# A scheduler that lets VectorE and GpSimd exclude each other, and an instruction order searched anew with it

## The chip, the core and the metric

The kernel runs on one core of one Trainium2 chip. The metric is the device time of one execution in microseconds (us). A core has five engines that run side by side and wait for each other through semaphores: TensorE (PE; its weight loads are shown apart as PEld), VectorE (DVE), ScalarE (ACT), GpSimd (POOL) and SyncE (SP), whose queue issues all DMAs of this kernel. The profile was taken in one execution; its span is the time from that execution's first instruction to its last.

## What is computed

An attention layer with soft-capped scores feeds a two-layer feed-forward block with a squared ReLU.

```python
scores = cap * tanh(scale * q @ k.T / cap)        # batch 4, heads 12, seq 448, head_dim 64
attn   = softmax(scores)                          # the row maximum is subtracted first
x      = (attn @ v) as [1792, 768]
h      = x @ w_in                                 # w_in [768, 2048]
g      = s * relu(h) ** 2 + b
out    = g @ w_out                                # w_out [2048, 768]
```

## The kernel before, in words

The work is cut into four batches j = 0 to 3 of 448 tokens. For each batch, attention runs over six pairs of heads. For a pair, TensorE computes blocks of scores (L505, into `ps_s`), ScalarE applies tanh (L509) and exp (L513), and TensorE multiplies the probabilities by the values and sums them (L563 and L571, into `ps_v`). ScalarE copies the result out (L591, `pw`), four small DMAs gather the row sums (L526, `cmp`), GpSimd and VectorE take their reciprocal (L534, L535, L538), a DMA writes it to DRAM (L540, `zd`), two DMAs read it back spread over partitions (L545), and one product (L437 on GpSimd) makes `num`, the reciprocal product. After six pairs a maximum is taken (L451, L609, L610), sent through TensorE so that all partitions have it (`lanes`, L470, one matmul of a single column), and x is split into a high half-precision part and a low part (L426 or L427, then L446).

The feed-forward weights arrive as 64-bit floats. VectorE rearranges their bits (L655, L656), an engine multiplies by a power of two (`expo`, L429 on GpSimd), and VectorE joins the bits (L659). Squares of the input weights (L693, L694 or L695, one instruction for each of three pieces of a column group) are summed by 12 small matmuls (`norm`, L705); a `lanes` matmul and a short VectorE sequence (`fin`, L721 to L726) give the scale, and the weights are split into high and low parts too. The output weights go the same way in `wout`; their column sums (L436 or L437) end in one matmul (L778).

The first product (L835, L836, L837) makes 16 blocks of 18 matmuls for each batch, the second (L1086 to L1088) six blocks of 48 for batches 0 and 1. Batches 2 and 3 use a form with fewer products (L995). After each block of the first product, ScalarE applies relu and square (L848, L853), a conversion makes the high part (`ghi`, L429 on GpSimd) and a subtraction the low part (`glo`, L437 on GpSimd).

No order is written by hand. Every instruction group is registered with a cost for each engine that may run it, a rank, its inputs and outputs. `Plan.emit` then plays the program through a model of the five engines and emits the groups in the order in which that model starts them; each engine executes its own part strictly in that order. The ranks come from the table `CHOICE["at"]`, the engines that an operation may use from entries such as `'expo'` or `'glo'`. Operations registered with `port=True` disturb each other in the model when VectorE and GpSimd run them at the same time:

```python
        loss = {"DVE": 0.9, "POOL": 0.7}
...
            if e in port and self.more[i][0]:
                other = port["POOL" if e == "DVE" else "DVE"]
                dur += max(0.0, min(other - t, dur)) * loss[e]
                port[e] = t + dur
```

Of the kernel before, what the change touches and what calls it, by code (L numbers as in the profile page):

```python
# [23 lines left out]
class Plan:  # L24
# [55 lines left out]
    def emit(self):  # L80
        n = len(self.ops)
# [31 lines left out]
        busy = {}  # L113
# [10 lines left out]
        shy = CHOICE["shy"]  # L124
        cold = 0.0
        kind = 0
        cling = CHOICE["cling"]

        def when(i, eng):
            ways, _, r, w, _ = self.ops[i]  # L130
            late = self.more[i][1]
            t = busy[eng]
            if eng == "SP" and len(landed) >= 8:
                t = max(t, landed[-8] - 0.4)
            for d in deps[i]:
                if start[d] is None:
                    return None
                t = max(t, end[d] + (0.0 if ran[d] == eng == "PE" else after[ran[d]] + before.get(eng, 0.0) + late))
# [4 lines left out]
            for p, ks in need.items():  # L143
                h, c = head[p], len(free[p])
                if set(order[p][h:h + len(ks)]) != ks:
                    return None
                for x in range(h, h + len(ks)):
                    if free[p][x % c] is None or taken.get((p, x % c)):
                        return None
                    t = max(t, free[p][x % c])  # L150
            for e, (dur, _) in ways.items():
                if e != eng and max(busy[e], t) + dur + shy.get(e, 0.0) + self.bias < t + ways[eng][0] + shy.get(eng, 0.0):
                    return None
            return t

        moved = 0.0
        landed = []
        port = {"DVE": 0.0, "POOL": 0.0}
        loss = {"DVE": 0.9, "POOL": 0.7}
        out = []  # L160
        todo = n
        while todo:
            best = None
            for reach in (80, n):
                for e, q in queue.items():
                    pick = None
                    for i in q[:reach]:
                        if pick and pick[0] <= busy[e] and self.ops[i][1] > self.ops[pick[1]][1] + cling:
                            break
                        t = when(i, e)  # L170
# [17 lines left out]
            t, i, e = best  # L188
            ways, _, r, w, move = self.ops[i]
            for other in ways:  # L190
                queue[other].remove(i)
            dur = ways[e][0]
# [18 lines left out]
            if e in port and self.more[i][0]:  # L211
                other = port["POOL" if e == "DVE" else "DVE"]
                dur += max(0.0, min(other - t, dur)) * loss[e]
                port[e] = t + dur
# [23 lines left out]
def arrange(units, at):  # L238

    key = {}  # L240
    for name, pre, _ in units:
# [4 lines left out]
CHOICE = {  # L246
    'bias': 1.798,
    'shy': {'DVE': 0.3, 'POOL': 0.5},
# [31 lines left out]
    },  # L280
    'alias': 2,
    'direct': 6,
    'cslag': 21,
    'late': 0.56,
    'lag': 0.0,
    'cling': 21.776,
    'parts': ((0, 1), (2, 3)),
# [5 lines left out]
    'sq': ('ACT', 'DVE', 'POOL'),  # L293
    'expo': ('POOL',),
    'whi': ('ACT', 'DVE'),
    'ohi': ('POOL',),
    'xhi': ('ACT', 'DVE'),
    'xmul': ('POOL',),
    'relu': ('ACT',),
    'gsq': ('ACT',),  # L300
    'glo': ('POOL',),
    'ghi': ('POOL',),
    'ehi': ('ACT', 'DVE', 'POOL'),
# [15 lines left out]
def attention_moe_kernel(  # L319
# [196 lines left out]
    def normal(bb, c2, rank):  # L516
# [19 lines left out]

        gps(0.4, rank, whole, r=["guard", *((kc, h, i) for h in range(2) for i in range(2))], w=[kc])
        dve(0.32, rank, lambda: nc.vector.reciprocal(P[kc][:, 0], P[kc][:, 0]), w=[kc])  # L538
# [14 lines left out]
    def pv(bb, c2, rank, step):  # L553
# [54 lines left out]
        def gather():  # L608
# [5 lines left out]
            gather,  # L614
            r=[("xm", bb, c) for c in range(NP)], w=[("xn", bb)],
        )
# [62 lines left out]
    def win(g, rank):  # L679
# [47 lines left out]

        dve(1.75, rank, fin, r=[kl], w=[("wnm", g), ("wc", g)])
        for c in range(NC3):
# [13 lines left out]
    def wout(d, rank):  # L743
# [44 lines left out]
        def amax():  # L788
# [4 lines left out]
        dve(  # L793
            0.68, rank, amax, r=[("wc", g) for g in range(NG)] + [("om", d, q) for q in range(NQ)], w=[("om", d)]
        )
# [5 lines left out]

        dve(1.3, rank, fin, r=[kl], w=[("op", d), ("os", d)])
        half = NQ // 2
# [60 lines left out]
    def mix(p, rank, step):  # L864
# [10 lines left out]

        dve(0.6, rank, scales, r=[("os", x) for x in d], w=[("ms", p)])
        for e in range(2):
# [379 lines left out]
```

## Time and profile before

| | before |
|---|---|
| median of 3 runs | 644.26 us (644.21 to 645.55) |
| the profiled execution, its own time | 644.03 us |
| its span | 642.2 us |
| PE busy | 627.1 us, 98% |
| DVE busy | 397.6 us, 62% |
| ACT busy | 326.6 us, 51% |
| POOL busy | 273.8 us, 43% |
| mean granted TensorE clock | 0.997 of full speed |

Busy time is the time in which an engine executes; what is missing to the span is idle time. The time of an execution is longer than its span by what lies around the first and the last instruction, here 1.83 us.

### The profile page before, as it was taken

What the parts mean: (1) busy time and instruction counts of PE and PEld (TensorE: products, weight loads), DVE (VectorE), ACT (ScalarE), POOL (GpSimd) and SP (SyncE); (2) the same over time, 40 slices, a digit from 0 to 9 for tenths busy, and PEclk for the clock granted to TensorE, in tenths of its full rate; (3) what the DMA queues carried; (4) which work ended last, traced back from release to release, by engine and by line L of the source; (5) the groups of instructions that cost most, each with busy time, mean ns of one, the idle gap of its engine ahead of it and who ended that gap; (6) DMA issues with size and microseconds to landing.
All of it is one profiled execution on the core that took longest, in us unless ns stands there. A gap on an engine that the chain in (4) does not pass through costs nothing.

```text
span 642.2 us, 11452 instructions
## 1 busy us (share of the span) xinstructions
PE 627.1 (98%) x4404; PEld 331.4 (52%) x4404; DVE 397.6 (62%) x778; ACT 326.6 (51%) x423; POOL 273.8 (43%) x319
## 2 busy tenths in 40 slices
PE   6999999999999999999999999999999999999997
PEld 2333344443334443333544445555558997556997
DVE  5896789997487787787400584745976222666222
ACT  5999987467866547537353561435544001434100
POOL 4553446885566568566343851112834001221000
PEclk9999999999999999989999999999999999999999
DMA  7767355441465674672800216676502875000672
GB/s 289 282 206 216 104 160 157 131 142 47 133 201 153 219 260 122 226 245 83 288 27 1 93 43 234 242 277 212 210 2 68 256 259 168 25 2 3 217 255 72
DMA packets 54775, 101.67 MB, mean 158 GB/s; under 512 B 16193, under 2 KB 34753, under 8 KB 54721
## 3 DMA queue, kind: packets, MB, share of 16 engines
q1 hardware_dynamic: 54720, 100.95, 47.1%
q8 instruction: 34, 0.56, 0.3%
q14 instruction: 21, 0.16, 0.1%
HBM read 82.58 MB, written 18.17 MB: 157 GB/s over the span
## 4 chain that ended last, share of the span: by engine, by line
PE 77%; DVE 8%; DMA 7%; POOL 3%; issue 2%; SPq 1%; ACT 0%; POOLq 0%; ACTq 0%
PE ps_m L995 9%; PE ps_s L505 7%; PE ps_s L995 6%; PE ps_v L563 6%; PE ps_s L836 6%; PE ps_s L837 6%; PE ps_s L835 6%; PE ps_m L1086 5%; PE ps_m L1088 5%; PE ps_m L1087 5%; PE ps_m L835 4%; PE ps_m L837 4%; PE ps_m L836 4%; PE ps_v L571 3%; DMA w<-in_w_in 2%
## 5 line engine op out<-in xcount | busy, mean ns | idle before, releaser
L995 PEld LDWEIGHTS <-w 128*128 128x128 f16 x1008 | 96.6, 98 | 0.7
L509 ACT ACTIVATE bed<-ps_s,arena 128x896 f32<-128x896 f32 x84 | 81.6, 1007 | 16.0 <-PE ps_s L505 14.8
L505 PE MATMUL ps_s<-bed 64*128 64x448 f32 (+1 forms) x384 | 82.7, 590 | 3.3 <-DMA bed<-in_qT 2.6
L513 ACT ACTIVATE bed<-bed,par 128x896 f32<-128x896 f32 x84 | 84.5, 1041 | 0.4
L563 PE MATMUL ps_v<-bed 128*32 128x448 f32 x768 | 82.2, 545 | 0.2 <-ACT pw L591 0.2
L1086 PE MATMUL ps_m<-gt,w 128*128 128x448 f16 x192 | 67.7, 353 | 0.0
L835 PE MATMUL ps_m<-x,w 128*128 128x448 f16 x192 | 67.7, 353 | 0.0
L836 PE MATMUL ps_s<-x,w 128*128 128x448 f16 x192 | 67.7, 352 | 0.0
L1088 PE MATMUL ps_m<-gt,w 128*128 128x448 f16 x192 | 67.7, 352 | 0.0
L837 PE MATMUL ps_m<-x,w 128*128 128x448 f16 x192 | 67.7, 352 | 0.0
L1087 PE MATMUL ps_m<-gt,w 128*128 128x448 f16 x192 | 67.7, 352 | 0.0
L835 PE MATMUL ps_s<-x,w 128*128 128x448 f16 x192 | 67.7, 352 | 0.0
L837 PE MATMUL ps_s<-x,w 128*128 128x448 f16 x192 | 67.7, 352 | 0.0
L836 PE MATMUL ps_m<-x,w 128*128 128x448 f16 x192 | 67.7, 352 | 0.0
L835 PEld LDWEIGHTS <-w 128*128 128x128 f16 x384 | 37.6, 98 | 38.7 <-issue 4.2
L837 PEld LDWEIGHTS <-w 128*128 128x128 f16 x384 | 37.6, 98 | 35.1
L836 PEld LDWEIGHTS <-w 128*128 128x128 f16 x384 | 37.6, 98 | 33.7
L429 POOL TENSOR_SCALAR w<-w 128x512 f32<-128x512 f32 x42 | 35.0, 833 | 40.0 <-DVE w L656 31.9
L930 ACT ACTIVATE pw<-ps_s,arena 128x448 f32<-128x448 f32 x32 | 20.3, 633 | 60.9 <-PE ps_s L837 57.8
L505 PEld LDWEIGHTS ps_s<-bed 64*128 64x128 f32 (+1 forms) x384 | 27.3, 177 | 45.4 <-issue 15.8
L437 POOL TENSOR_TENSOR pw<-pw 128x224 f32<-128x224 f32 x16 | 13.7, 860 | 79.5 <-ACT pw L934 63.1
L563 PEld LDWEIGHTS ps_v<-bed 128*32 128x32 f32 x768 | 20.5, 109 | 52.4 <-issue 38.6
(138 smaller groups left out, 1065.3 us busy)
## 6 DMA issues: line engine op xcount, KB each, us to landing
w<-w SPq DMA_DIRECT2D x48, 512.0 KB, 5.5
w<-in_w_out SPq DMA_DIRECT2D x24, 512.0 KB, 5.5
w<-ws SPq DMA_DIRECT2D x24, 512.0 KB, 4.7
w<-in_w_in SPq DMA_DIRECT2D x18, 512.0 KB, 5.4
bed<-in_v SPq DMA_DIRECT2D x24, 256.0 KB, 3.5
ws<-w SPq DMA_DIRECT2D x12, 512.0 KB, 2.9
bed<-in_kT SPq DMA_DIRECT2D x24, 224.0 KB, 3.8
bed<-in_qT SPq DMA_DIRECT2D x24, 224.0 KB, 3.8
```

What stands on the lines that cost most here:

```text
L429: 0.1 + n * 0.00107, lambda: nc.gpsimd.tensor_scalar(dst(), src(), sc, 1.0, ALU.mult, ALU.mult)
L505: nc.tensor.matmul(P[kp][o, h, 0:S], keys, P[q][rows], start=True, stop=True)
L509: 1.01, rank, lambda: nc.scalar.activation(P[kh], P[kp][:, :, 0:S], AF.Tanh, scale=tsc[:, 0:1]),
L513: 1.04, rank, lambda: nc.scalar.activation(P[kh], P[kh], AF.Exp, scale=par[:, 0:1]), r=["par"], w=[kh],
L563: nc.tensor.matmul(P[kp][o, 0, 0:S], P[kv][:, c, o], prob(c, h), start=(c == 0), stop=(c == NC))
L835: nc.tensor.matmul(ps[:, 0:S], wh, x[:, 0], start=(c == 0), stop=False)
L836: nc.tensor.matmul(ps[:, 0:S], wh, x[:, 1], start=False, stop=False)
L837: nc.tensor.matmul(ps[:, 0:S], wl, x[:, 0], start=False, stop=(c == NP - 1))
L995: nc.tensor.matmul(at(), w(g, zw), b(g, zb), start=g == 0 and x == 0, stop=g == n - 1 and x == 2,)
L1086: nc.tensor.matmul(ps[:, 0:S], wh, ghi[:, f], start=(f == 0), stop=False)
L1087: nc.tensor.matmul(ps[:, 0:S], wh, glo[:, f], start=False, stop=False)
L1088: nc.tensor.matmul(ps[:, 0:S], wl, ghi[:, f], start=False, stop=(f == NF - 1))
```

## The change

The model's charge for two disturbing operations is replaced. An operation with `port=True` that starts while the other engine's last such operation still runs is now held up until that one's end, less 0.15 us, and then takes its full own time. The choice between engines counts this hold-up too, and the scheduler looks through the whole queue of ready work where it looked at the first 80 entries first. Five more groups of operations are marked `port=True`. Four kinds of operation may run on more engines than before, and the table of ranks and three numbers beside it are new. What the instructions compute is the same.

```diff
-            for e, (dur, _) in ways.items():
-                if e != eng and max(busy[e], t) + dur + shy.get(e, 0.0) + self.bias < t + ways[eng][0] + shy.get(eng, 0.0):
-                    return None
+            if len(ways) > 1:
+                own = ways[eng][0] + held_up(i, eng, t)
+                for e, (dur, _) in ways.items():
+                    at = max(busy[e], t)
+                    if e != eng and at + dur + held_up(i, e, at) + shy.get(e, 0.0) + self.bias < t + own + shy.get(eng, 0.0):
+                        return None
             return t
+
+        def held_up(i, e, t):
+            if e not in port or not self.more[i][0]:
+                return 0.0
+            return max(0.0, port["POOL" if e == "DVE" else "DVE"] - t - 0.15)
...
-        loss = {"DVE": 0.9, "POOL": 0.7}
...
-            for reach in (80, n):
+            for _ in range(1):
                 for e, q in queue.items():
                     pick = None
-                    for i in q[:reach]:
+                    for i in q:
...
-                other = port["POOL" if e == "DVE" else "DVE"]
-                dur += max(0.0, min(other - t, dur)) * loss[e]
+                dur += held_up(i, e, t)
...
-    'bias': 1.798,
+    'bias': 1.806,
...
-        ('a', 0, 0): (-15.1, 72.6), ('a', 0, 2): (69.2, 7.69), ('a', 0, 4): (78.0, 15.05), ('a', 1, 0): (600.1, 1.25),
+        ('a', 0, 0): (-88.4, 62.61), ('a', 0, 2): (80.2, 2.4), ('a', 0, 4): (227.3, 40.55),
...
-    'late': 0.56,
+    'late': 0.621,
-    'cling': 21.776,
+    'cling': 19.274,
...
-    'expo': ('POOL',),
+    'expo': ('DVE', 'POOL'),
-    'ohi': ('POOL',),
+    'ohi': ('ACT', 'DVE', 'POOL'),
-    'xmul': ('POOL',),
+    'xmul': ('DVE', 'POOL'),
-    'glo': ('POOL',),
-    'ghi': ('POOL',),
+    'glo': ('DVE', 'POOL'),
+    'ghi': ('ACT', 'DVE', 'POOL'),
...
-        dve(1.75, rank, fin, r=[kl], w=[("wnm", g), ("wc", g)])
+        dve(1.75, rank, fin, r=[kl], w=[("wnm", g), ("wc", g)], port=True)
```

The diff makes the file longer by 7 to 8 lines, so that a line number of the kernel before stands 7 to 8 higher in the rows of the changed kernel below.

TensorE executes the same 4404 matmul records as before. GpSimd executes 81 instructions fewer, ScalarE 49 and VectorE 32 more. The larger moves are these: of 32 conversions `gt<-r` (`ghi`) on GpSimd 23 go to ScalarE and 4 to VectorE; of 32 subtractions `gt<-r,gt` (`glo`) on GpSimd 19 go to VectorE; of 48 high parts of the output weights (`ohi`) on GpSimd 19 go to ScalarE and 7 to VectorE; of 48 `expo` products on GpSimd 10 go to VectorE; of 24 reciprocal products on GpSimd 7 go to VectorE.

Three places show how the order moves. The first is the beginning of the SP queue, from its first DMA on (`in_kT` and `in_qT` are the keys and queries of one pair of heads, `par` holds the three scalars of the input). Before:

```order
L1132 DMA par<-in_cap 128x1
L481 DMA bed<-in_kT 128x448
L483 DMA bed<-in_qT 128x448
L647 DMA w<-in_w_in 128x1024 x3
L1132 DMA par<-in_s 128x1
L1132 DMA par<-in_b 128x1
L481 DMA bed<-in_kT 128x448
L483 DMA bed<-in_qT 128x448
L487 DMA bed<-in_v 128x512
L647 DMA gt<-in_w_in 128x1024
```

In the changed kernel, from the same instruction on:

```order
L1140 DMA par<-in_cap 128x1
L488 DMA bed<-in_kT 128x448
L490 DMA bed<-in_qT 128x448
L654 DMA w<-in_w_in 128x1024 x3
L488 DMA bed<-in_kT 128x448
L490 DMA bed<-in_qT 128x448
L1140 DMA par<-in_s 128x1
L1140 DMA par<-in_b 128x1
L494 DMA bed<-in_v 128x512 x2
L654 DMA gt<-in_w_in 128x1024
```

The keys and queries of the second pair have moved ahead of the two scalars s and b, and the second load of values ahead of a piece of weights.

The second place is VectorE's work just before it reads the third `norm` result (the third L713, which becomes L720). Before, with the bit join of the last piece (L659) and the squares (L694):

```order
L655 TENSOR_SCALAR gt<-gt 128x512
L656 SCALAR_TENSOR_TENSOR gt<-gt 128x512
L538 RECIPROCAL cmp<-cmp 128x7
L659 SCALAR_TENSOR_TENSOR gt<-gt 128x512
L451 TENSOR_REDUCE arena<-num 128x1
L694 TENSOR_TENSOR bed<-w 128x512 x2
L713 TENSOR_REDUCE arena<-ps_m 128x1
```

In the changed kernel (L662, L663, L434 and L666 are the bit work with its product, L701 the square):

```order
L662 TENSOR_SCALAR gt<-gt 128x512
L663 SCALAR_TENSOR_TENSOR gt<-gt 128x512
L434 TENSOR_SCALAR gt<-gt 128x512
L545 RECIPROCAL cmp<-cmp 128x7
L666 SCALAR_TENSOR_TENSOR gt<-gt 128x512
L701 TENSOR_TENSOR bed<-gt 128x512
L701 TENSOR_TENSOR bed<-w 128x512 x2
L720 TENSOR_REDUCE arena<-ps_m 128x1
```

The power-of-two product and the square of the last piece `gt`, both on GpSimd before, now stand on VectorE between its own instructions.

The third place is on TensorE, where the `lanes` matmul of batch 1 (L470, which becomes L477) stands. Between the last value matmul of batch 1 and this one stood 18 first-product matmuls, nine score blocks and four value steps of later pairs; the last of them are shown:

```order
L505 MATMUL ps_s<-bed 128x448 x2
L563 MATMUL ps_v<-bed 32x448 x8
L571 MATMUL ps_v<-bed,ones 32x448
L571 MATMUL ps_v<-bed,half 32x448
L571 MATMUL ps_v<-bed,ones 32x448
L571 MATMUL ps_v<-bed,half 32x448
L505 MATMUL ps_s<-bed 128x448 x2
L470 LDWEIGHTS ones_132
L470 MATMUL ps_m<-brief,ones_132 128x1
L835 LDWEIGHTS w_6_127
L835 MATMUL ps_m<-x,w_6_127 128x448
```

In the changed kernel 36 matmuls of the first product (L842 to L844 and their like, of which the last is shown) stand directly ahead of it:

```order
L845 LDWEIGHTS w_6_127
L845 MATMUL ps_m<-x,w_6_127 128x448
L477 LDWEIGHTS ones_132
L477 MATMUL ps_m<-brief,ones_132 128x1
L512 MATMUL ps_s<-bed 128x448 x2
L785 MATMUL ps_m<-arena,bed 128x1
L512 MATMUL ps_s<-bed 128x448 x2
L477 LDWEIGHTS ones_132
L477 MATMUL ps_m<-brief,ones_132 128x1
```

Between the last value matmul of batch 1 and this one now stand 144 first-product matmuls, eight score blocks (a row of four is two blocks of two) and two value steps. The column sum of the first output block (L778, now L785) follows it after one score block.

## Rows read from the trace of the kernel before

**Rows 1.** Stretches: length, busy PE, PEld, DVE, ACT, POOL; clock, DMA, GB/s

```profile
0.00:14.00 14.00, 9.16 (x34) 3.24 (x38) 6.44 (x11) 6.75 (x8) 5.52 (x16) 1.00 0.75 271
14.00:80.00 66.00, 64.14 (x556) 21.20 (x552) 51.98 (x116) 61.73 (x70) 31.25 (x40) 1.00 0.65 209
80.00:180.00 100.00, 98.87 (x694) 42.06 (x694) 82.87 (x162) 72.14 (x96) 64.23 (x71) 1.00 0.43 135
180.00:310.00 130.00, 126.02 (x863) 50.41 (x856) 104.39 (x225) 75.46 (x84) 85.99 (x112) 0.99 0.56 183
310.00:638.00 328.00, 328.00 (x2263) 213.84 (x2262) 151.43 (x264) 110.52 (x168) 86.81 (x82) 1.00 0.41 141
638.00:642.20 4.20, 0.91 (x10) 0.66 (x7) 0.45 (x1) 0.00 (x0) 0.00 (x0) 1.00 0.21 79
```

**Rows 2.** TensorE's own waits: for whom, us in total, times, longest

```profile
PE ps_m L778 <- POOL bed L437: 2.5, 1, 2.5
...
PE ps_m L470 <- DVE brief L715: 0.8, 2, 0.5
```

**Rows 3.** Timeline, 3.5 to 14 us, with what ended the idle time before

```profile
3.54 0.44 SPq L1132 DMA_DIRECT2D par<-in_s  x1
4.03 0.63 SPq L1132 DMA_DIRECT2D par<-in_b  x1
...
5.40 0.43 SPq L483 DMA_DIRECT2D bed<-in_qT  x1
...
12.50 0.97 PE L505 MATMUL ps_s<-bed 64*64 64x448 f32 x4 [1.93 <-DMA bed<-in_qT]
...
13.40 1.71 PE L563 MATMUL ps_v<-bed 128*32 128x448 f32 x16
```

**Rows 4.** DMA throughput in 40 slices of 0.5 us, from 0 to 20 us

```profile
GB/s 0 0 0 0 36 90 165 381 391 363 385 426 401 401 410 401 164 49 4 259 373 387 433 431 417 392 397 417 433 418 418 410 393 410 418 381 389 377 405 418
```

**Rows 5.** Timeline around the third sum of squares, 60 to 68 us

```profile
60.12 0.70 DVE L659 SCALAR_TENSOR_TENSOR gt<-gt 128x512 int32<-128x512 int32 x1
...
64.11 1.15 POOL L437 TENSOR_TENSOR num<-pw,bed 128x448 f32<-128x448 f32 x1
...
64.20 1.60 DVE L659 SCALAR_TENSOR_TENSOR gt<-gt 128x512 int32<-128x512 int32 x1 [0.46 <-POOL gt L429]
...
65.95 1.04 POOL L695 TENSOR_TENSOR bed<-gt 128x512 bf16<-128x512 f32 x1 [0.69 <-DVE gt L659]
...
67.05 0.35 PE L705 MATMUL ps_m<-ones,bed 128*128 128x1 bf16 x8 [1.24 <-POOL bed L695]
```

**Rows 6.** Timeline of TensorE at the lanes matmul of batch 1

```profile
183.72 0.16 PE L470 MATMUL ps_m<-brief,ones 128*128 128x1 bf16 x1 [1.41 <-DVE brief L610]
183.75 0.35 PE L835 MATMUL ps_m<-x,w 128*128 128x448 f16 x1
183.94 0.35 PE L836 MATMUL ps_m<-x,w 128*128 128x448 f16 x1
```

**Rows 7.** The chain that ended last, at 42 and 275 us: start, us, what

```profile
41.61 1.71 PE ps_s L505 x8
43.31 1.64 PE ps_v L563 x16
...
45.71 1.87 PE ps_s L505 x12
...
274.72 3.27 PE ps_s L505 x12
```

**Rows 8.** The stretch behind the wait of 2.45 us, columns as in Rows 1

```profile
274.90:278.40 3.50, 3.50 (x16) 0.70 (x12) 3.13 (x13) 1.37 (x2) 2.23 (x5) 0.51 0.67 181
```

**Rows 9.** Groups of instructions: shapes, count, busy us, mean ns, idle before

```profile
L436 DVE TENSOR_TENSOR gt<-pw,gt 128x448 f16<-128x448 f32 x23 | 14.7, 639 | 3.2 <-ACT gt L426 2.6
...
L437 POOL TENSOR_TENSOR gt<-r,gt 128x448 f16<-128x448 f32 x32 | 38.3, 1200 | 1.2
...
L426 ACT ACTIVATE gt<-pw 128x448 f16<-128x448 f32 x11 | 6.1, 572 | 4.5 <-POOL pw L437 2.8 <-DVE pw L436 1.2 <-PE ps_m L1088 0.3
```

More of the change, by code (lines that the diff above doesn't have):

```diff
@@ L535, in whole @@
             nc.gpsimd.tensor_scalar(a, a, guard[:, 0:1], 0.0, ALU.add, ALU.add)
-        gps(0.4, rank, whole, r=["guard", *((kc, h, i) for h in range(2) for i in range(2))], w=[kc])
+        gps(0.55, rank, whole, r=["guard", *((kc, h, i) for h in range(2) for i in range(2))], w=[kc], port=True)
         dve(0.32, rank, lambda: nc.vector.reciprocal(P[kc][:, 0], P[kc][:, 0]), w=[kc])
@@ L614, in pv @@
             gather,
-            r=[("xm", bb, c) for c in range(NP)], w=[("xn", bb)],
+            r=[("xm", bb, c) for c in range(NP)], w=[("xn", bb)], port=True,
         )
@@ L793, in wout @@
         dve(
-            0.68, rank, amax, r=[("wc", g) for g in range(NG)] + [("om", d, q) for q in range(NQ)], w=[("om", d)]
+            0.68, rank, amax, r=[("wc", g) for g in range(NG)] + [("om", d, q) for q in range(NQ)], w=[("om", d)],
+            port=True,
         )
@@ L800, in fin @@
             nc.vector.tensor_scalar(sc, wn, si, None, ALU.mult)
-        dve(1.3, rank, fin, r=[kl], w=[("op", d), ("os", d)])
+        dve(1.3, rank, fin, r=[kl], w=[("op", d), ("os", d)], port=True)
         half = NQ // 2
@@ L874, in scales @@
             nc.vector.tensor_scalar(rs, iswo[:, d[0]:d[1] + 1], top[:, 0:1], None, ALU.mult)
-        dve(0.6, rank, scales, r=[("os", x) for x in d], w=[("ms", p)])
+        dve(0.6, rank, scales, r=[("os", x) for x in d], w=[("ms", p)], port=True)
         for e in range(2):
```

59 rows, old and new, of the table CHOICE are left out of this document.

## The prediction

> **What bounds the kernel now.** I read the busy time by stretch first [rows 1]. TensorE is busy for 328.00 of 328 us from 310 to 638 us: there the kernel can't get faster by a change of order. Before 310 us it stands still for little: 14 - 9.16 = 4.84 us in the first 14 us, then 1.86, 1.13 and 3.98 us in the next three stretches (66 - 64.14, 100 - 98.87, 130 - 126.02), and 4.20 - 0.91 = 3.29 us at the very end. The sum is 15.10 us. The busy time itself is dense: in the first product one matmul starts 0.19 us after the other [rows 6]. TensorE executes the same 4404 matmuls after the change, so only these 15.10 us can shrink, and what a stall costs afterwards through the clock. The same rows show what the other engines can spare: ScalarE is busy 61.73 of 66 us in the second stretch, and 72.14 of 100 in the third; VectorE 82.87 of 100 in the third.
>
> Next come the waits of TensorE themselves. In the head, the score block that serves the rest of the sequence of two pairs together waits 1.93 us for the second pair's queries, which were issued at 5.40 us behind the two scalars s and b [rows 3]. Around 8 to 9.5 us the DMA engines move 164, 49 and 4 GB/s where they move about 400 before and behind [rows 4]. The third sum of squares waits 1.24 us for a square on GpSimd [rows 5]. The lanes matmul of batch 1 waits 1.41 us [rows 6]. The column sum of one output block waits 2.45 us, shown rounded as 2.5 [rows 2], and behind it the granted clock stands at 0.51 of full speed for 3.5 us, which is the lower of the two levels, 1.2 GHz [rows 8]; 12 score matmuls take 3.27 us there that take 1.87 elsewhere [rows 7], so that this stall has a second price of 1.40 us. The mid waits are 1.86 + 1.13 + 3.98 = 6.97 us; with the clock 8.37.
>
> **How VectorE and GpSimd meet.** The wait of 1.24 us can be followed back [rows 5]. The bit join L659 takes 0.70 us at 60.12. At 64.20 it takes 1.60: a GpSimd product that began at 64.11 runs until 65.26, so 1.06 us of it are left. The new charge gives 0.70 + 1.06 - 0.15 = 1.61 us, the old one 0.70 + 0.9 x 0.70 = 1.33. The new one is right here, the old one 0.27 us too low; the square on GpSimd starts after the join and TensorE after the square. The Trainium skill (SBUF — State Buffer, section "SBUF: two separate sides") says that the two engines share a port pair as an exclusive lock: the one that starts first keeps it for its whole instruction. The trace agrees in this place, 1.60 us. By that rule alone every such collision is foreseen by the new model and the 3.82 us that I keep below would go, ending at 635.8; by the rows they stay, since only this one wait is traced to a collision.
>
> **The change part by part.**
>
> The head. Keys and queries of the second pair go ahead of s and b. If the slow 1.5 us belong to the two scalars, the scores no longer wait: -1.93 us. But the first values now stand behind both scalars, and the value matmuls, which began at 13.40 [rows 3], need them. Two loads of 128 x 448 numbers of four bytes at 400 GB/s take 1.15 us; 8.0 + 1.15 + 1.5 + 0.65 for 128 x 512 values gives 11.3 as the earliest start, 13.40 as the latest. I take the middle, -0.9 us (bounds -1.93 and 0).
>
> The third sum of squares. The product and the square of the late piece stand on VectorE, no hand-over to GpSimd is left, and the square stands ahead of two others that the sum doesn't need. -1.24 us (bound 0, if that VectorE chain is late).
>
> The lanes matmul of batch 1. Before, there lay 18 x 0.19 + 9 x 0.855 + 4 x 2.40 = 20.7 us of TensorE work between the last values and it (a score block is half of 1.71 us; a value step with its sums lasts from 43.31 to 45.71 [rows 7]), and it was 1.41 us too little. Now it is 144 x 0.19 + 8 x 0.855 + 2 x 2.40 = 39.0 us. -1.41 us (bound 0).
>
> The rest of the mid waits and the clock: 8.37 - 1.24 - 1.41 = 5.72 us, at places such as the column sums and the lanes matmuls [rows 2]. All 32 groups of this sort (18 lanes, 8 sums of squares, 6 column sums) stand elsewhere now, so this is drawn again. The bounds are 0 and the whole 5.72. The model's view of collisions is better; its view of DMAs, which end other such chains, is the old one. I let two thirds stay: 3.82 us, a gain of 1.90.
>
> New waits that the rows let me price. The first lanes matmul has two score blocks ahead of it since its sum of squares, 1.71 us, where a value step stood there too; three short VectorE steps fit, but one long one such as L659 at 0.70 to 1.60 us more does not: 0 to 1.3 us, I take 0.5. For the 49 instructions that ScalarE gets I take another 0.5 us: in the third stretch ten conversions of 0.572 us [rows 9] and some six others of about 0.6 come to 9.4 us on top of 72.14 of 100, which leaves it room on average but not at each place (bounds 0 and the second rival). Together +1.0.
>
> The low parts cost nothing on the path: 19 subtractions leave GpSimd at 1.200 us for VectorE at 0.639 [rows 9], which covers them with idle time of 17.13 us in the third stretch and 25.61 in the fourth [rows 1]; if that cover were gone, each would delay a second product by at most 0.639. Freed time on GpSimd is worth something only where a wait ends on it. After 310 us no stall is there to remove, and with 176.57 us idle on VectorE of 328 I see none to add: 0. The end is the same code with the same last block: 0.
>
> The sum: -0.9 - 1.24 - 1.41 - 1.90 + 1.0 = -4.45 us on the span of 642.2 gives 637.75, and with the 1.83 us that lie around it 639.6 us. (The profiled execution's own time, 644.03, lies 0.23 under the median of 644.26.) No more than 1.93 + 8.37 = 10.30 can come off: 631.9 + 1.83 = 633.7 us is the floor.
>
> **The rivals.**
>
> Nothing gained but the head. The new order loses at its own places what the old one lost at its own, 8.37 us with the clock, since waits of this kind come mostly from DMA chains whose price didn't change: the wait of batch 1, for one, is the end of a chain of three DMAs. Then -0.9 to 0 remain: 643.1 to 644.0 us. For it: only 1.24 of 6.97 us is traced to a collision. Against it: 39.0 us of cover in place of 20.7 is in the program, whatever the model thought.
>
> ScalarE becomes late (slower). Its relu frees the two PSUM buffers of the first product, and the ten conversions of batch 0 now run on the same engine between tanh and exp of the attention. It decides from the point where ScalarE work ahead of a relu is longer than one block of matmuls, 18 x 0.19 = 3.4 us: then TensorE stands. If half of the ten conversions come through, 2.9 us, and two of these stalls bring the clock down, 2 x 1.40, the span is 5.7 us longer than in the rival above: 649 us, and 646 with a quarter of them and one clock drop. Against it: 18.5 us are still idle of 100.
>
> The planner's new order is much better than I grant: all of 8.37 and 1.5 of the head go, 632.3 + 1.83 = 634.2 us.
>
> **How the numbers follow.** I call a difference within 0.2%, 1.3 us, no change: what a measurement of this kernel can just tell. The forecast has a chance of 0.62, ScalarE late 0.12, nothing but the head 0.19, everything gone 0.07. The forecast's own range comes from its bounds: the third of the drawn term could be all or nothing (-3.8 to +1.9), the head -1.0 to +0.9: 636.4 to 642.6. The range of 8 in 10 leaves out below it the last rival, and above it the longer half of ScalarE's: 636.4 to 645.0. Faster holds the forecast, the last rival and a little of the rival that ends at 643.1 (the border is 642.97): 0.70. Same holds most of that rival: 0.17. Slower 0.13.
>
> **What would show it.** In the changed profile: no wait of TensorE for the queries in the first 14 us, and value matmuls before 13.4 us; no wait at the third sum of squares and none at the lanes matmul of batch 1; mid waits of 3 to 5 us in place of 6.97 by the stretch table, and one clock drop or none; long VectorE steps seldom over twice their own time. It is wrong if waits before 310 us sum to 6 us or more, if relu on ScalarE ends TensorE's waits, or if TensorE stands still between 310 and 638 us.

## The result, and the profile after

The changed kernel takes **638.57 us** (median of 19 runs, 635.98 to 644.37), the kernel before 644.52 us in the same series (19 runs, 641.89 to 648.27): a ratio of 0.9917 with a 95% interval of 0.9898 to 0.9936. The profiled execution took 639.61 us and spans 637.8 us, 4.4 us less than the one before. The medians lie further apart, by 5.95 us. A difference that the two profiles don't show is how often the clock drops: the mean granted clock of each execution is on record, and one drop to half for 3.4 us in some 640 makes it 0.997. It is 0.997 or less in 52 of 68 executions of the kernel before (taken beside e1 to e12, one slow one left out), and in 8 of 25 of the changed kernel (this series and e11). Both profiled executions are among these. In the series of the changed kernel the five executions with such a drop have a median of 641.48 us, the other fourteen 638.46. All lines of the changed kernel that the prediction named stand some 7 lines further down (L705 is L712, L470 is L477, L778 is L785).

The stretches, to be read against [rows 1] (length, busy time of PE, PEld, DVE, ACT, POOL, then clock, DMA share, GB/s):

```profile
0.00:14.00 14.00, 10.02 (x46) 3.49 (x50) 6.38 (x12) 7.43 (x9) 4.26 (x14) 1.00 0.81 293
14.00:80.00 66.00, 63.27 (x527) 20.19 (x519) 53.69 (x113) 58.91 (x67) 29.24 (x35) 0.97 0.65 204
80.00:180.00 100.00, 100.00 (x700) 43.64 (x693) 77.08 (x190) 81.57 (x112) 40.27 (x49) 1.00 0.41 134
180.00:310.00 130.00, 129.19 (x914) 51.23 (x912) 106.13 (x237) 84.48 (x103) 67.21 (x83) 1.00 0.59 184
310.00:634.00 324.00, 324.00 (x2233) 212.61 (x2232) 156.46 (x259) 119.28 (x185) 67.13 (x59) 1.00 0.43 144
634.00:637.80 3.80, 0.53 (x6) 0.27 (x3) 0.45 (x1) 0.00 (x0) 0.00 (x0) 1.00 0.14 50
```

TensorE's idle time is 3.98, 2.73, 0, 0.81, 0 and 3.27 us, 10.79 in all; before it was 4.84, 1.86, 1.13, 3.98, 0 and 3.29, 15.10. The difference of 4.31 us is the difference of the spans but for 0.1. So the gain lies in 80 to 310 us (4.30 us) and the head (0.86), and 14 to 80 us lost 0.87. GpSimd is busy 40 instead of 64 us in the third stretch, ScalarE 82 instead of 72.

TensorE's waits, to be read against [rows 2] (for whom, us in total, times, longest):

```profile
PE ps_m L1163 <- POOL w L1166: 2.1, 1, 2.1
PE ps_m L712 <- DVE bed L701: 1.7, 1, 1.7
PE ps_s L512 <- DMA bed<-in_qT: 1.6, 2, 1.0
PE ps_m L785 <- DVE bed L443: 0.8, 2, 0.6
PE ps_v L570 <- ACT pw L598: 0.6, 1, 0.6
PE ps_s L512 <- ACT bed L516: 0.3, 1, 0.3
PE ps_m L477 <- DVE brief L722: 0.3, 1, 0.3
```

The first of them, 2.08 us at the very start for a GpSimd memset, is as long in the kernel before. Of the column sums one waited 2.45 us; now two wait, 0.23 and 0.58. The largest wait behind the start is now the third sum of squares, 1.66 us against 1.24 [rows 5]; the granted clock falls behind it:

```profile
59.73 0.43 DVE L662 TENSOR_SCALAR gt<-gt 128x512 int32<-128x512 int32 x1 [1.71 <-DMA gt<-in_w_in]
...
61.91 1.14 POOL L444 TENSOR_TENSOR num<-pw,bed 128x448 f32<-128x448 f32 x1
62.00 1.62 DVE L666 SCALAR_TENSOR_TENSOR gt<-gt 128x512 int32<-128x512 int32 x1
...
63.77 1.04 POOL L702 TENSOR_TENSOR bed<-gt 128x512 bf16<-128x512 f32 x1 [0.72 <-DVE gt L666]
64.05 1.05 DVE L662 TENSOR_SCALAR gt<-gt 128x512 int32<-128x512 int32 x1
...
66.01 1.20 POOL L702 TENSOR_TENSOR bed<-w 128x512 bf16<-128x512 f32 x1
...
66.37 1.39 DVE L666 SCALAR_TENSOR_TENSOR gt<-gt 128x512 int32<-128x512 int32 x1
...
67.79 0.69 DVE L701 TENSOR_TENSOR bed<-gt 128x512 bf16<-128x512 f32 x1
...
68.54 0.35 PE L712 MATMUL ps_m<-ones,bed 128*128 128x1 bf16 x8 [1.66 <-DVE bed L701]
```

```profile
69.80:73.20 3.40, 3.40 (x19) 0.50 0.56 159
```

The first fence is the timeline of the chain that feeds the sum, the second the stretch behind it (busy PE, clock 0.50, the lower level of 1.2 GHz). Three steps of VectorE run beside a GpSimd product or square that had begun shortly before: 1.62, 1.05 and 1.39 us, where the same forms take 0.69 (L666, in e4 below) and 0.43 (L662, first line) alone. That is 0.93 + 0.62 + 0.70 = 2.25 us on one unbroken chain of VectorE, more than the 1.66 that TensorE waits. How much of it could be had back is tested for the last one alone (e4): in e3 the second of these steps also waits for its load, until 63.98 us.

The lanes matmul of batch 1 no longer waits: its operand is ready at 165.43 us, and it runs at 172.02; before, TensorE waited 1.41 us for it at 183.72 [rows 6].

```profile
165.27 0.16 DVE L617 CAST brief<-arena 128x1 bf16<-128x1 f32 x1
...
172.02 0.17 PE L477 MATMUL ps_m<-brief,ones 128*128 128x1 bf16 x1
```

In the head the queries of the second pair still wait, 0.96 in place of 1.93 us, and the value matmuls start at 12.39 in place of 13.40 [rows 3]; the DMA engines (slices of 0.5 us from 0 to 20) no longer fall to 4 GB/s [rows 4], only to 194 in one slice at 9.5:

```profile
11.49 0.97 PE L512 MATMUL ps_s<-bed 64*64 64x448 f32 x4 [0.96 <-DMA bed<-in_qT]
12.39 0.96 PE L570 MATMUL ps_v<-bed 128*32 128x448 f32 x8
```

```profile
GB/s 0 0 0 0 51 47 172 366 399 335 385 402 393 393 393 434 368 398 325 194 355 375 406 414 383 396 410 400 355 251 430 401 401 426 418 418 397 391 402 436
```

### The profile page after: what moved, and what is told of

The parts are those of the page before. It is cut to its first block, busy times and chain, and to the rows that moved or that the text cites. A ratio compares the mean times of both kernels' runs of the same rounds, so it can differ in the third digit from the quotient of the medians.

```text
span 637.8 us, 11435 instructions
## 1 busy us (share of the span) xinstructions
PE 627.0 (98%) x4404; PEld 331.4 (52%) x4404; DVE 400.2 (63%) x810; ACT 351.7 (55%) x472; POOL 208.1 (33%) x238
## 4 chain that ended last, share of the span: by engine, by line
PE 85%; DMA 8%; DVE 3%; ACT 1%; SPq 1%; POOL 1%; issue 0%; ACTq 0%
PE ps_v L570 9%; PE ps_m L1003 9%; PE ps_s L512 7%; PE ps_s L1003 6%; PE ps_m L843 6%; PE ps_s L844 6%; PE ps_m L844 6%; PE ps_s L843 6%; PE ps_m L845 6%; PE ps_s L845 6%; PE ps_m L1094 5%; PE ps_m L1095 5%; PE ps_m L1096 5%; PE ps_v L578 4%; DMA gt<-in_w_in 2%; DMA w<-in_w_out 2%
## 5 line engine op out<-in xcount | busy, mean ns | idle before, releaser
L512 PE MATMUL ps_s<-bed 64*128 64x448 f32 (+1 forms) x384 | 80.6, 578 | 1.9 <-DMA bed<-in_qT 1.6
L844 PE MATMUL ps_s<-x,w 128*128 128x448 f16 x192 | 67.7, 353 | 0.0
L844 PE MATMUL ps_m<-x,w 128*128 128x448 f16 x192 | 67.7, 353 | 0.0
L844 PEld LDWEIGHTS <-w 128*128 128x128 f16 x384 | 37.6, 98 | 33.8
L444 POOL TENSOR_TENSOR pw<-pw 128x224 f32<-128x224 f32 x24 | 21.6, 912 | 77.6 <-ACT pw L942 71.2
L578 PE MATMUL ps_v<-bed,ones 128*32 128x448 f32 x288 | 45.5, 545 | 0.0
```

The lines of the kernel that those rows point to most:

```text
L512: nc.tensor.matmul(P[kp][o, h, 0:S], keys, P[q][rows], start=True, stop=True)
L578: nc.tensor.matmul(P[kp][o, 1, 0:S], w, ph, start=first, stop=last)
L844: nc.tensor.matmul(ps[:, 0:S], wh, x[:, 1], start=False, stop=False)
```

## The experiments

Two theories stood against each other. Mine: the gain is TensorE's order at a few places, found by a search in the new model, and each wait stands by itself. The rivals: the model alone does it; the wider choice of engines does it; waits taken away come back. Where a run moves single instructions, the scheduler's finished order is edited by index pairs: (x, y) puts instruction group x right behind group y. In the kernels the pairs stand in the loop itself; here they are called PAIRS.

```diff
+        for x, y in PAIRS:
+            out.remove(x)
+            out.insert(out.index(y) + 1, x)
         for i in out:
```

**e1 and e2: the two scalars.**

```diff
-            512, -80 + i if i else -100, lambda i=i, a=a: nc.sync.dma_start(par[:, i:i + 1], a.to_broadcast([128, 1])),
+            512, 10 + i if i else -100, lambda i=i, a=a: nc.sync.dma_start(par[:, i:i + 1], a.to_broadcast([128, 1])),
```

That is e1, in the kernel before; e2, in the changed kernel, has -85 in place of 10.

> The kernel before, with the loads of the scalars s and b issued behind the second pair's keys and queries; no instruction of any other queue changes its place. Theory 'the scalars hold up the queue': no stretch of under 50 GB/s at 8 to 9.5 us, the wait for the second pair's queries falls from 1.93 us to about 1.0, the value matmuls start at about 12.4 us in place of 13.40, and the time falls by 0.9 to 1.0 us (ratio 0.9985). Rival 'the slow stretch belongs to the two scalars wherever they stand and the values inherit it': values at 13.4 us, time unchanged. Rival 'the head is made up for later': values at 12.4 us, time unchanged.

> The changed kernel, with s and b put back ahead of the second pair's keys and queries; nothing else moves. Theory 'the scalars hold up the queue': the slow stretch is back, the wait for the queries grows from 0.96 to about 1.9 us, the values start at about 13.4 us, the time grows by 0.9 to 1.0 us (ratio 1.0015). Rival 'the new order has slack behind the head': the wait is back, but the time stays within 0.2 us of the changed kernel.

Measured: e1 644.54 us, ratio to before 0.9993 (0.9972 to 1.0015); e2 639.09 us, 0.9916 (0.9892 to 0.9941). A microsecond is too little for the times, so only the traces can say something, and they show the head alone: whether the rest of the kernel makes its microsecond up later stays open. DMA throughput in the same slices, e1 and then e2:

```profile
GB/s 0 0 0 0 33 72 169 376 385 302 393 402 377 377 361 442 376 405 335 112 107 314 422 406 415 388 411 410 449 418 410 426 401 426 373 397 379 391 407 407
```

```profile
GB/s 0 0 0 0 58 58 147 330 368 368 401 410 393 369 361 451 287 58 23 227 377 412 402 413 455 414 382 401 396 393 411 410 401 401 434 410 410 394 373 394
```

The trough moves with the scalars, from 8 us to 9.5 and back, and where they come later it is shallower (lowest 107 in e1, 23 in e2). In e1 the wait for the queries falls to 0.46 us and the values start at 12.71 (0.69 us earlier, 0.41 us of waiting for the first value load included); in e2 it is 1.32 and the values start at 13.07. So the head is worth 0.7 to 1.0 us. e2 has no drop of the clock, and spans 636.7 us in spite of its head: one execution of the changed kernel differs from the next by as much as this edit.

**e3 and e4: the third sum of squares.** e3 moves it on TensorE, e4 only takes a GpSimd square (the one at 66.01 above) out of the way.

```diff
+PAIRS = (184, 364), (185, 323), (186, 535), (187, 186)   # e3: sum; its maximum; lanes matmul; what reads it
+PAIRS = (293, 242),                                      # e4: square of a later group behind cmp
```

> The changed kernel, with the third sum of squares behind the value step that follows it, its lanes matmul behind the next two score blocks; no other matmul changes its place. Theory 'a stall costs its own length and the clock behind it': the 1.66 us at 68.5 us and the 3.4 us at half speed behind it go together, the time falls by 1.66 + 1.4 to 1.7 = 3.1 to 3.4 us (ratio 0.995). Rival 'the clock falls anyway, at the next small wait': 1.66 us (0.9974). Rival 'the chain behind this sum is what is late': the wait comes back at the lanes matmul or at the first product that needs this group, 0 to 0.5 us (0.9995).

> The changed kernel, with one square on GpSimd (of a later group, begun at 66.01 us) behind the two short GpSimd instructions that follow it; the order of TensorE, VectorE, ScalarE and SP is the same. Theory 'the port': the bit join on VectorE that ran beside it, 1.39 us at 66.37, takes 0.70, the third sum of squares waits about 0.97 us in place of 1.66, the time falls by 0.7 us, or by some 2 us if the clock then stays up (ratio 0.999 to 0.997). Rival 'the piece's transfer is late, the port is not': the wait stays at 1.66 us, the time does not change.

Measured: e3 639.56 us, 0.9921 (0.9899 to 0.9944): nothing gained. e4 638.38 us, 0.9899 (0.9874 to 0.9925). The timelines, e3 first:

```profile
70.62 1.40 DVE L701 TENSOR_TENSOR bed<-w 128x512 bf16<-128x512 f32 x1
...
72.32 0.16 DVE L722 CAST brief<-arena 128x1 bf16<-128x1 f32 x1
72.53 0.16 PE L477 MATMUL ps_m<-brief,ones 128*128 128x1 bf16 x1 [1.19 <-DVE brief L722]
```

```profile
65.83 0.69 DVE L666 SCALAR_TENSOR_TENSOR gt<-gt 128x512 int32<-128x512 int32 x1
...
66.56 0.69 DVE L701 TENSOR_TENSOR bed<-gt 128x512 bf16<-128x512 f32 x1
...
67.31 0.35 PE L712 MATMUL ps_m<-ones,bed 128*128 128x1 bf16 x8 [0.28 <-DVE bed L701]
```

In e3 the sum waits no longer and the clock stays up, but the step that reads it now stands on VectorE behind a square that takes 1.40 us (by my pair (185, 323)), and the lanes matmul waits 1.19 us; later waits of 1.10 and 0.68 us end on column sums. That is what the third theory said, though here it is the place that my pair gave to that step. In e4 the join takes 0.69 us instead of 1.39, with no other change on its engine, the wait falls from 1.66 to 0.28 us, the clock stays up, and the span is 635.4 us. So the collision is worth 0.70 of the 1.38 us; the rest is this execution's, in which the chain's first step, L662, starts 0.52 us earlier (59.21 for 59.73) and TensorE comes to the sum 0.16 later. The size is that of the exclusion: the square had 66.01 + 1.20 - 66.37 = 0.84 us to run, and 0.84 - 0.15 + 0.69 = 1.38. The Trainium skill (SBUF — State Buffer, section "SBUF: two separate sides") says that a GpSimd step that reads SBUF and a VectorE step with two SBUF inputs, as the join has, exclude each other: whichever starts first keeps the shared port pair for its whole instruction. The trace agrees, 1.39 us beside the square and 0.69 without it. By its median e4 can't be told from the changed kernel (638.57), so this gain is shown in the trace alone. None of the six executions of e4 has a clock of 0.997 or less.

**e5, e6 and e7: model, table and engines apart.** e5 runs the new CHOICE in the old scheduler, e6 the old CHOICE in the new one (so e6 lacks the wider choice of engines too), e7 the changed kernel with the edit below. The section on the change counts four kinds of operation with a wider choice and five more groups with `port=True`; by the diff they are five and six, and one of the six has its cost raised from 0.4 to 0.55 us.

```diff
-    'expo': ('DVE', 'POOL'),
+    'expo': ('POOL',),
...
-    'ghi': ('ACT', 'DVE', 'POOL'),
+    'ghi': ('POOL',),
```

> The old scheduler (its loss factors, its reach of 80, its old port marks) with the new table, constants and choice of engines. Theory 'the order is made of table and model together; a table draws waits afresh in any model it wasn't searched in': TensorE's waits between 14 and 310 us are as large as before or larger, 6 to 12 us, time 642 to 650 us. Rival 'the table and the wider choice of engines carry the gain, the model only guided the search': 3 to 4 us of waits, 637 to 640 us.

> The new scheduler (exclusion, its port marks, no reach) with the old table, constants and choice of engines. Theory 'the order is made of table and model together': waits between 14 and 310 us of 6 to 12 us, time 642 to 650 us. Rival 'the better model avoids collisions by itself': waits fall to 3 to 5 us, 638 to 641 us.

> The changed kernel with the five kinds of conversion and product (expo, ohi, xmul, glo, ghi) back on GpSimd alone; model, table and constants stay the new ones. Theory 'order counts, the engine of a conversion hardly': up to the first places where the order changes the waits are those of the changed kernel, then drawn afresh, 638 to 644 us. Rival 'the work taken off GpSimd is what pays': GpSimd's long products end TensorE's waits again, 643 to 650 us. Rival 'no part of the gain hangs on these': 638.0 to 639.2 us.

Measured: e5 747.79 us, ratio 1.1586 (1.1533 to 1.164); e6 646.67 us, 1.0015 (0.9989 to 1.0041); e7 650.30 us, 1.0074 (1.005 to 1.0098). TensorE's longest waits of e5, e6, e7:

```profile
PE ps_s L836 <- ACT pw L931: 27.1, 5, 12.3
PE ps_s L506 <- ACT bed L510: 11.4, 8, 2.0
```

```profile
PE ps_s L511 <- ACT bed L515: 3.7, 4, 1.6
PE ps_v L569 <- ACT bed L519: 2.9, 1, 2.9
```

```profile
PE ps_m L477 <- DVE brief L722: 3.7, 3, 2.5
PE ps_m L785 <- DVE bed L443: 3.4, 3, 1.9
```

Neither half carries the gain. The new model on the old numbers draws as many waits as the old one, in other places (the attention's tanh and exp are late). The new numbers in the old model are far worse than I expected, with single waits of up to 12.3 us for ScalarE's relu of batches 2 and 3 (L931). And the new model and numbers without the wider choice of engines make a kernel that is 0.7% slower than before, where I had expected 638 to 644 us; its waits end on VectorE and ScalarE far more than on GpSimd. The rival "the better model avoids collisions by itself" falls, and so does "no part hangs on the engines".

**e9: the engines back, the order kept.** The order of e7 is another one, so its time doesn't tell what the engines are worth. Here 89 instructions go back to GpSimd, each at its place:

```diff
-            self.ops[i][0][ran[i]][1]()
+            self.ops[i][0]['POOL' if i in BACK else ran[i]][1]()
```

> The changed kernel in its own order, but the 89 instructions of the five kinds (expo, ohi, xmul, glo, ghi) that it gave to VectorE and ScalarE run on GpSimd again, each at its old place in the sequence. Theory of the prediction 'low parts and conversions are covered by idle time, order is what pays': TensorE's waits before 310 us within 1 us of those of the changed kernel, 638 to 640 us. Rival 'an order made for three engines needs the three engines': GpSimd, about 100 us busier, is late for the products that read its conversions, waits of 5 us or more, 643 us or slower.

Measured: 644.26 us, 0.9984 (0.9957 to 1.0011), beside 640.55 for the changed kernel on the same chip (e11). The whole gain is gone. GpSimd is nowhere full (58.91 of 100 us in the third stretch); the waits end on VectorE, whose steps now wait for GpSimd first. Waits, VectorE's row maxima of `num` with their idle time (in e9, then in e11), and the timeline at the third sum:

```profile
PE ps_m L785 <- DVE bed L443: 2.6, 2, 1.6
PE ps_m L712 <- DVE bed L701: 2.3, 1, 2.3
```

```profile
L458 DVE TENSOR_REDUCE arena<-num 128x1 f32<-128x448 f32 x21 | 12.9, 615 | 19.0 <-POOL num L444 19.0
L458 DVE TENSOR_REDUCE arena<-num 128x1 f32<-128x448 f32 x21 | 12.8, 613 | 6.2 <-POOL num L444 6.1
```

```profile
66.35 0.65 POOL L436 TENSOR_SCALAR gt<-gt 128x512 f32<-128x512 f32 x1
...
66.96 1.03 POOL L702 TENSOR_TENSOR bed<-w 128x512 bf16<-128x512 f32 x1
67.03 1.52 DVE L666 SCALAR_TENSOR_TENSOR gt<-gt 128x512 int32<-128x512 int32 x1 [0.41 <-POOL gt L436]
```

The product on GpSimd frees GpSimd for the next square just as VectorE wants to join, and the join loses its turn by 0.07 us, which costs it 0.83 us. This is one place; the longer waits at the column sums were not followed to a single cause. Ten of the twelve executions of e9 have a clock of 0.997 or less, so that part of the 3.7 us is probably the clock's.

**e8 and e12: the kernel before, three places moved.** Both have the edit of e1; e8 moves the third sum behind a score block and a value step, e12 only behind the score block; both move the lanes matmul of batch 1.

```diff
+PAIRS = (184, 462), (185, 184), (186, 504), (187, 186), (694, 709)   # e8
+PAIRS = (184, 478), (694, 709)                                       # e12
```

> The kernel before, with its old model and table, and three edits of order: s and b behind the second pair's keys and queries, the third sum of squares behind the next score block and value step (its lanes matmul two score blocks later), the lanes matmul of batch 1 behind the first half of a block of the first product. No instruction changes its engine. Theory 'what the change gained is TensorE's order at a few places, whatever the model': the waits of about 1.0 us (of 1.93), 1.24 and 0.8 to 1.4 us go, time 640.9 to 641.5 us (ratio 0.995). Rival 'each wait taken away comes back at the next consumer of the same chain': 644 us.

> The kernel before with s and b behind the second pair's keys and queries, the third sum of squares behind one score block (and not behind the value step, so that no buffer of its squares is given on before it), and the lanes matmul of batch 1 behind half a block of the first product. Theory 'TensorE's order at a few places pays, whatever the model': 0.95 of 1.24 us, 0.8 to 1.4 and about 1 us go, 641.3 to 642.2 us (ratio 0.996). Rival 'waits come back': 644 us.

Measured: e8 645.86 us, 1.0003 (0.9977 to 1.0028); e12 642.31 us, 0.9964 (0.9949 to 0.9978). In e8 two buffers of the sum's squares had been planned for later squares, which were now written first, so that its third sum reads squares of later groups; and the squares that wait for the sum hold up ScalarE:

```profile
71.13 0.67 ACT L693 ACTIVATE bed<-w 128x512 bf16<-128x512 f32 x1 [3.93 <-PE ps_m L705]
...
73.68 1.86 PE L505 MATMUL ps_s<-bed 64*128 64x448 f32 x4 [1.69 <-ACT bed L509]
```

In e12, without that, the wait of the sum is 0.19 us and that of batch 1 gone, and TensorE's order does pay in the old model too: 2.5 us under the median of before. Not all of this need come from the three places: none of its twelve executions has a clock of 0.997 or less, where 19 of the 23 of before have, and the column sum, which was not moved, waits 1.34 us in place of 2.45. Even so it is less than the 4.58 us of the three waits, since two new ones of 1.1 and 1.2 us end on ScalarE (at 29.7 and 76.7 us).

**e10 and e11: what is left.** e10 is a version that should beat both kernels: the square of e4, the two scalars, a bit pass, and three column sums with what reads them. e11 is the changed kernel again.

```diff
+PAIRS = (293, 242), (1, 39), (2, 1), (295, 25), (802, 1229), (803, 806), (912, 1420), (913, 916), (967, 1515), (968, 971)
```

> The changed kernel with six places moved: the GpSimd square of e4, s and b behind the first two value loads, one bit pass on VectorE behind the step that feeds the first lanes matmul, and three column sums (for the bias alone) behind the next score block or value step. Theory 'what is left between the head and 310 us are single waits that can be covered one by one': waits of 1.66, 0.3, 0.2 and 0.6 us go, 0.7 us or so of the head, and the drop of the clock; 635.5 to 637 us, 1.5 to 3 us under the changed kernel run beside it (e11). Rival 'each covered wait comes back at the next consumer': within 0.7 us of e11.

> The changed kernel itself, to be compared with e10 on the same chip, and to see how its waits differ between two executions: ratio 0.990 to 0.993; the wait of the third sum of squares again 1.4 to 1.7 us; the drop of the clock behind it may be there or not. A theory that 'the waits of one profile are fixed' expects each within 0.1 us of the first profile.

Measured: e10 636.93 us, 0.9889 (0.9866 to 0.9912); e11 640.55 us, 0.9928 (0.9901 to 0.9954). The medians are 3.6 us apart, and the intervals just overlap: faster than before for certain, than the changed kernel probably. In e10's stretches TensorE has no idle time from 180 to 310 us, and the third sum waits 1.0 us, while the head gained nothing:

```profile
0.00:14.00 14.00, 9.69 (x42) 3.39 (x46) 6.28 (x12) 7.27 (x8) 3.96 (x14) 1.00 0.82 272
180.00:310.00 130.00, 130.00 (x916) 51.45 (x914) 106.93 (x240) 84.41 (x104) 65.69 (x83) 1.00 0.58 189
```

```profile
PE ps_s L512 <- DMA bed<-in_qT: 1.9, 2, 1.2
PE ps_m L712 <- DVE bed L701: 1.0, 1, 1.0
```

The head stands idle for 4.31 us where the changed kernel had 3.98 and e11 4.07, and a new wait of 0.84 us for ScalarE stands at 28.8 us. Before 310 us the idle time is 4.31 + 2.99 + 0 + 0 = 7.30 us, little under the 7.52 of the changed kernel's first profile (8.99 in e11). What e10 surely lacks is the drop: none of its five executions has a clock of 0.997 or less. At the third sum it repeats e4: VectorE's chain starts at 61.09 us as in e11 (61.16), the same square is out of the way, and the wait is 1.01 us against 1.67.

In e11 the third sum waits 1.67 us, again with a drop of the clock behind it. A wait of 1.1 us for ScalarE at 49.6 us is new to the same program:

```profile
PE ps_s L512 <- ACT bed L516: 1.1, 1, 1.1
```

## Why the prediction was right, and where it wasn't

The time (639.6 for 638.57) and the sum (-4.45 on the span for -4.4) are right; two of its terms are not, and their errors cancel. That is luck, and so is how close the sum came: both profiled executions had a drop of the clock, and the medians differ by 5.95 us. The ends of the forecast's own range don't follow from its bounds either: added up, -3.8 and -1.0 give 634.8, and 1.9 and 0.9 give 642.4.

- **The head, -0.9.** Right in size: 0.86 us less idle, values 1.01 earlier; e1 and e2 show that the two scalars make the trough, and that their place is worth 0.7 of the 1.01. Its inner working was half wrong: the queries wait still (0.96 us), and the values, which were to be late behind the scalars, wait for nothing in this execution and 0.4 in e11.
- **The third sum of squares, -1.24.** This step failed: "no hand-over to GpSimd is left" is so, but the chain on VectorE was late, the bound that I had named and not taken. It meets three GpSimd products on the way, 2.25 us. The wait is 0.42 us longer than before, and the clock fell behind it. e4 removed one of the three and the wait fell to 0.28.
- **The lanes matmul of batch 1, -1.41.** Right; it has 6.6 us to spare, and moved alike in the kernel before (e12) it doesn't wait either.
- **The rest of the mid waits and the clock, 5.72, two thirds to stay.** Mis-sized. Without the third sum, the first lanes matmul and the wait on pw, 3.54 - 1.66 - 0.31 - 0.59 = 0.98 us of waits are left of 4.32; with a drop of the clock of 3.4 us at half speed (1.40 before; at most 1.7 now) 2.4 to 2.7 in place of 3.82. The new order left less of these waits than I granted it. The clock's part stayed in this execution; over all on record it shrank, from 52 of 68 with a drop to 8 of 25.
- **New waits, +1.0.** 0.31 at the first lanes matmul for 0.5, and 0.59 for ScalarE's copy of pw for 0.5: right, if by another instruction of ScalarE than the conversions that I had in mind.
- **Low parts 0, freed GpSimd time worth nothing.** Wrong as a reason. No wait of TensorE ends on a moved instruction where they are now, though two of them stand in VectorE's chain at the third sum (a `num` product of 0.63 us at 60.80, the power-of-two product of 0.47 at 65.87); and e9 shows that the new order stands on them: back on GpSimd they cost 3.7 us, not because GpSimd is busy all the time but because VectorE's steps wait for its products (19.0 us before the row maxima for 6.1) and, at the one place that was followed, collide with them.
- **After 310 us and the end, 0.** Right: 324.00 of 324, and 3.27 us for 3.29.

Of the rivals, "ScalarE becomes late" didn't come: no wait of TensorE ends on the relu. It is what happens in e5 (27.1 us on L931); in e6 ScalarE is late with tanh and exp. Of the signs, the mid waits are 3.54 us, inside 3 to 5; my limit of 6 us was meant for these, but as it is written, for all waits before 310 us, it was passed: with the head the sum is 7.52. Two more signs failed, no wait for the queries and none at the third sum. "Long VectorE steps seldom over twice their own time" failed just on the chain that mattered.

What stays open: what the exclusion in the model is worth by itself. No order was searched anew in the old model with the wider choice of engines, so a second search might have found as much; the runs show only that this table needs this model. The largest single gain, at the column sums, was not taken apart either: the one that waited 2.45 us waits 1.87 in e1 and 1.34 in e12, where it was not moved. Open too is how much of the 0.2 to 0.7 us by which single waits differ between executions comes from the DMAs, which start at other times in each; no run here holds them fixed.

## What to carry to other kernels

An order found by search belongs to the model and the choice of engines it was found with: without the engines the kernel is no faster than before (e9, order kept) or 0.7% slower (e7), without the model 16% slower (e5), without the new numbers and engines no faster (e6), where all together gain 0.8%. So such a change is to be judged as a whole, by the waits of the engine that bounds the kernel. To cover a wait, look at what the moved instruction releases as well as at what it waits for: in e3 and e8 the wait came back one step later. And keep loads of a few bytes per partition out of a queue's head while large ones that the first matmuls need are still to come.

## What the runs showed of the hardware

- Two loads of 128 x 4 bytes ahead of large ones leave the DMA engines nearly without work for more than a microsecond (164, 49, 4 GB/s in slices of 0.5 us before; 287, 58, 23 in e2), where neighbouring slices move about 400. Behind the second pair's keys and queries they cost less: 112 and 107 in e1, 194 in the changed kernel.
- The bit passes of VectorE (L662, L666) that started while a GpSimd product or square ran took their own time and what the other had left, less 0.15 us: 1.62, 1.05 and 1.39 us (changed kernel) and 1.52 (e9), where this sum gives 1.59, 1.04, 1.38 and 1.50. Not every step is held: the reciprocal L545 took 0.18 us at 66.24 us, beside the square that began at 66.01.
- The length of a wait alone does not decide whether the clock falls behind it: it fell to half for 3.4 us behind waits of 2.45 us (before), 1.66 and 1.67 (the changed kernel, twice), and stayed up behind 1.87 us (the column sum of e1), 1.45 (the third sum of e2) and 2.88 (e6, at 82 us). The same program has the drop in some executions and not in others (8 of 25 of the changed kernel).
- Two executions of one program (the changed kernel and e11) differ by a wait of 1.1 us that only one of them has, and by 2.1 us of span; differences below that are read from a named wait, not from a span.
